# The up product's second pass on the two row halves of the TensorE array

## The chip, the cores and the metric

One core of a Trainium2 chip runs the kernel, in one launch. The metric is the device time of that launch in microseconds (us). The kernel before was run three times: 2138.86, 2139.70 and 2140.49 us, with a median of 2139.7 us.

## The reference

Four batches of 12480 queries, keys and values with 128 channels attend through 49 agents; the result, 49920 tokens of 128 channels, goes through a feed-forward layer with 2048 hidden values:

```
a2k = softmax(scale * agents @ k.T)        # 49 x 12480, per batch
agent_v = a2k @ v                          # 49 x 128
q2a = softmax(scale * q @ agents.T)        # 12480 x 49
x = q2a @ agent_v                          # 12480 x 128
h = x @ w_in                               # 128 -> 2048
out = (h * sigmoid(1.702 * h)) @ w_out     # 2048 -> 128
```

All of it is float32 (the feed-forward weights come as float64).

## The kernel before, in words

The kernel never forms `x`. Per batch it multiplies `agent_v` and `w_in` beforehand (`agent_weights`, L289 to L309): the product, 49 x 2048, is the weight matrix of the up product, and the queries' probabilities over the agents are its moving operand. The 49 agents are padded to 64 rows (`H`), and the weights stand twice on the 128 partitions, in rows 0 to 63 and again in rows 64 to 127.

To keep float32's accuracy with TensorE's `float32r` operands, values are split in an upper and a lower part. The weights become `wh` and `wl` (L307, L308). The probabilities of a group of 960 tokens, in two chunks of 480, become `sa` for the first chunk and `sb` for the second (`query_pairs`, L336 to L354). In `sa` the upper parts lie in rows 0 to 63 and the lower parts in rows 64 to 127; in `sb` it is the other way round. So one matmul over 128 rows sums upper and lower parts against the same weights.

The main loop (L540) has 4 batches x 13 groups x 16 blocks of 128 hidden values, 832 steps in all. A step is:

- `up`, four matmuls of 128 rows, 128 columns of weights and 480 columns of moving data: `wh` against `sa` and `sb` (L362), then `wl` against `sa` and `sb` (L364), summed in two PSUM tiles `ph`, one for each chunk. ScalarE applies the gate (L369) to give `g`; ScalarE or VectorE makes its upper part `gh` (L371, L373), VectorE the lower part `gl` (L374).
- `down`, for the block of four steps earlier (`LAG`), six matmuls of the same size (L385): `wo_h` against `gh`, `wo_h` against `gl`, `wo_l` against `gh`, for each chunk, summed in `po` over the 16 blocks.

So a step has ten matmuls of 128 x 128 x 480, each with its own load of 128 x 128 weights. Beside the steps, at fixed blocks of a group, come the next group's query scores (bfloat16 matmuls, L182 to L185), transposes of the probabilities (L345), and for the next batch key scores, key maxima (`key_max`, with the transposes L235 and L241) and key-value products (L272). L241 takes 49 rows and is one of only four matmuls of the kernel before with so few rows; the program gives it a tile of 64 x 128 of the array. The transpose L235 and the first batch's L489 have 49 columns of weights and a tile of 128 x 64; all others take 128 x 128.

The order on each engine is made by the tile scheduler from the order of the code and from the buffers. On TensorE the two matmuls of a line usually stand next to each other, but in some steps other work comes between. TensorE works through its instructions in the order of the program, and a weight load may run beside the matmul before it.

Of the kernel before, what the change touches and what calls it, by code (L numbers as in the profile page):

```python
# [20 lines left out]
CH = 480  # L21
# [21 lines left out]
def kernel(  # L43
# [10 lines left out]
    nc = tc.nc  # L54
# [6 lines left out]
    H = P // 2  # L61
# [9 lines left out]
    ps_o = ctx.enter_context(tc.tile_pool(name="ps_o", bufs=1, space=bass.MemoryType.PSUM))  # L71
    ps_m = ctx.enter_context(tc.tile_pool(name="ps_m", bufs=2, space=bass.MemoryType.PSUM))

# [1 line left out]
    ag_sb = const.tile([P, B, A], F32, name="ag_sb")  # L75
    nc.sync.dma_start(out=ag_sb, in_=agT)

    ident = const.tile([P, P], F32, name="ident")
    make_identity(nc, ident)
    # sel[k, m] = 1 where k and m name the same agent in either half  # L80
    sel = const.tile([P, P], F32, name="sel")
    nc.vector.memset(sel, 0.0)
    for c in range(2):
        nc.vector.tensor_add(
            out=sel[:, c * H : c * H + A], in0=ident[:, 0:A], in1=ident[:, H : H + A]
# [20 lines left out]
    part_max = const.tile([P, NKG, A], F32, name="part_max")  # L106
    max_b = const.tile([P, A], F32, name="max_b")

    # a float64's words, low then high, to the nearest float32; what is under
    # float32's range becomes zero and what is over it infinite  # L110
    def load_words(src, i):
        w = loads.tile([P, 512, 2], U32, name="words", tag="kv")
        nc.sync.dma_start(out=w.rearrange("p n w -> p (n w)"), in_=src[:, i * 1024 : (i + 1) * 1024])
        return w

    def to_float32(w, out=None):
        lo = w[:, :, 0]
        hi = w[:, :, 1]
        ts = nc.vector.tensor_scalar
        stt = nc.vector.scalar_tensor_tensor  # L120
        # 2 ** exponent, with the sign
        tmp = work.tile([P, 2, 512], U32, name="tmp", tag="rest")
        ex = tmp[:, 0].bitcast(I32)
        ts(out=ex.bitcast(U32), in0=hi, scalar1=20, scalar2=0x7FF, op0=ALU.logical_shift_right, op1=ALU.bitwise_and)
        ts(out=ex, in0=ex, scalar1=1023 - 127, scalar2=1023 + 128, op0=ALU.max, op1=ALU.min)
        ts(out=ex, in0=ex, scalar1=float(127 - 1023), scalar2=float(1 << 23), op0=ALU.add, op1=ALU.mult)
        stt(out=ex.bitcast(U32), in0=hi, scalar=0x80000000, in1=ex.bitcast(U32), op0=ALU.bitwise_and, op1=ALU.bitwise_or)
        # the mantissa's upper 45 bits as a whole number, rounded once
        m = work.tile([P, 512], U32, name="m21", tag="o")
        r = tmp[:, 1]  # L130
        ts(out=m, in0=hi, scalar1=0xFFFFF, scalar2=0x100000, op0=ALU.bitwise_and, op1=ALU.bitwise_or)
        ts(out=r, in0=lo, scalar1=8, scalar2=None, op0=ALU.logical_shift_right)
        stt(out=m.bitcast(F32), in0=m, scalar=float(1 << 24), in1=r, op0=ALU.mult, op1=ALU.add)
        if out is None:
            out = m.bitcast(F32)
        stt(out=out, in0=m.bitcast(F32), scalar=2.0**-44, in1=ex.bitcast(F32), op0=ALU.mult, op1=ALU.mult)
        return out

    def up_weights(i, w):
        to_float32(w, w_in_sb[:, i * 512 : (i + 1) * 512])  # L140

    def down_weights(i, w):
        s = slice(i * 4, (i + 1) * 4)
        wo = to_float32(w).rearrange("p (f c) -> p f c", c=C)
        nc.scalar.copy(out=wo_h[:, s, :], in_=wo)
        nc.vector.tensor_sub(out=wo_l[:, s, :], in0=wo, in1=wo_h[:, s, :].bitcast(F32))

    # ---- scores: a float32 is the sum of three bfloat16, and of the parts'
    # products all are summed but those under a float32 product's own rounding ----
    ag_part = const.tile([P, B, 3, A], BF16, name="ag_part")  # L150
    rest = ag_sb
    for i in range(3):
# [7 lines left out]
        w = t.bitcast(BF16).rearrange("p (n w) -> p n w", w=2)  # L160
        return w[:, :, 1], w[:, :, 0]

    # the upper half of a word is the first part; of what is left the upper
    # half is the second, and the third takes the place of the lower
    def split(t):
        r = work.tile([P, GT + PAD], F32, name="rest", tag="rest")
        nc.gpsimd.memset(t[:, GT:], 0.0)  # L167
        nc.gpsimd.tensor_sub(out=r, in0=t, in1=halves(t)[0])  # L168
        nc.gpsimd.tensor_sub(out=halves(r)[1], in0=r, in1=halves(r)[0])  # L169
        return halves(t)[0], halves(r)[0], halves(r)[1]  # L170
# [20 lines left out]
                nc.scalar.copy(out=o, in_=s[:, :, 0, :])  # L191
                nc.vector.tensor_add(out=o, in0=s[:, :, 1, :], in1=o)

# [1 line left out]
    def key_load(b, g):  # L195
        t = loads.tile([P, GT + PAD], F32, name="kt", tag="kv")
        nc.sync.dma_start(out=t[:, 0:GT], in_=kT[b, :, g * KB : (g + 1) * KB, :].rearrange("p j t -> p (j t)"))
        return t

    def first_key_scores(g, kt):  # L200
        # two batches' agents to a pass, as many columns as keep the clock up
        for c in range(2):
            ps = ps_m.tile([P, 512], F32, name="ps_m")
            for j in range(KB // 2):
                nc.tensor.matmul(  # L205
                    out=ps[:TB, j * 2 * A : (j + 1) * 2 * A],
                    lhsT=kt[:, c * KB // 2 + j, :],
                    rhs=ag_sb[:, 0:2, :].rearrange("p b a -> p (b a)"),
                    start=True,
                    stop=True,  # L210
                )
            s = ps[:TB, : KB * A].rearrange("p (j b a) -> p j b a", b=2, a=A)[:, :, 0, :]
            i = 2 * g + c
            nc.scalar.copy(out=score[:TB, i * KB // 2 : (i + 1) * KB // 2, :], in_=s)
        nc.vector.tensor_reduce(
            out=part_max[:TB, g, :],
            in_=score[:TB, g * KB : (g + 1) * KB, :].rearrange("p j a -> p a j"),
            axis=AX.X,
            op=ALU.max,
        )  # L220
# [87 lines left out]
            nc.vector.tensor_sub(out=wl[:, s], in0=pw, in1=wh[:, s].bitcast(F32))  # L308
        return wh, wl  # L309

# [1 line left out]
    def query_load(b, g):  # L312
        t = loads.tile([P, GT + PAD], F32, name="qt", tag="qt", bufs=2)
        nc.sync.dma_start(out=t[:, 0:GT], in_=qT[b, :, g * GT : (g + 1) * GT])
        return t
# [37 lines left out]
        nc.vector.tensor_sub(out=sb[0:H], in0=ps[H:P, :CH], in1=sb[H:P].bitcast(F32))  # L353
        return sa, sb  # L354

# [1 line left out]
    def up(f, wts, pairs):  # L357
        wh, wl = wts
        s = slice(f * P, (f + 1) * P)
        ph = [ps_h.tile([P, 512], F32, name="ph") for _ in range(2)]  # L360
        for c in range(2):
            nc.tensor.matmul(out=ph[c][:, :CH], lhsT=wh[:, s], rhs=pairs[c], start=True, stop=False)  # L362
        for c in range(2):
            nc.tensor.matmul(out=ph[c][:, :CH], lhsT=wl[:, s], rhs=pairs[c], start=False, stop=True)  # L364
        g = gpool.tile([P, 2, CH], F32, name="g")
        gh = gpool.tile([P, 2, CH], F32R, name="gh", bufs=LAG + 1)
        gl = gpool.tile([P, 2, CH], F32R, name="gl", bufs=LAG + 1)
        for c in range(2):
            nc.scalar.activation(out=g[:, c, :], in_=ph[c][:, :CH], func=AF.Gelu_apprx_sigmoid)  # L369
        if f in HI_ON_ACT:  # L370
            nc.scalar.copy(out=gh, in_=g)  # L371
        else:
            nc.vector.tensor_copy(out=gh, in_=g)  # L373
        nc.vector.tensor_sub(out=gl, in0=g, in1=gh.bitcast(F32))  # L374
        return gh, gl
# [21 lines left out]
            t0 = b * N + g * GT + c * CH  # L397
            nc.sync.dma_start(out=outT[:, t0 : t0 + CH], in_=o)

# [1 line left out]
    kts = {}  # L401
    vts = {}
    qts = {}
# [5 lines left out]
    pairs = {}  # L409
# [41 lines left out]
    def do_weights(b):  # L451
        wts[b] = agent_weights(accs.pop(b))

    # the first batch's keys and values have nothing to run beside, and lie
    # where the weights and the hidden values come to lie afterwards
    def first_keys():
        tags = [("g", 3), ("gh", LAG + 1), ("gl", LAG + 1)]
        tiles = []
        for tag, bufs in tags:
            tiles += [gpool.tile([P, KB, TB], F32, name="kt0", tag=tag, bufs=bufs) for _ in range(bufs)]  # L460
        return tiles[:NKG]
# [14 lines left out]
    words = [load_words(w_out, i) for i in range(NF // 4)]  # L476
    for g in range(NKG):
        first_key_scores(g, kts.pop((0, g)))
# [5 lines left out]
    for g in range(NKG):  # L484
# [3 lines left out]
        for j in range(KB):  # L488
            nc.tensor.matmul(  # L489
                out=acc_ps[:A, : C + 1],  # L490
                lhsT=score[:TB, g * KB + j, :],
                rhs=vt[:TB, j, :],
                start=(g == 0 and j == 0),
                stop=(g == NKG - 1 and j == KB - 1),
# [10 lines left out]
    do_weights(0)  # L505
    down_weights(0, words[0])

    # what is done for the next batch beside a group: in steps of the group's
    def beside(b, g):
        jobs = {}  # L510
        if b == 0 and g == 0:
# [25 lines left out]
    steps = B * NG * NF  # L537
# [70 lines left out]
```

## Time and profile before

| | us |
|---|---|
| median of three runs | 2139.7 |
| profiled execution, first to last instruction | 2139.6 |
| PE (TensorE matmul) busy | 2083.2 |
| PEld (TensorE weight load) busy | 1777.1 |
| DVE (VectorE) busy | 1865.0 |
| ACT (ScalarE) busy | 1611.9 |
| POOL (GpSimd) busy | 519.8 |

The profiled execution's own time is the span of 2139.6 us; the median of the runs is the same within 0.1 us. Busy time on PE is the time covered by matmul records. A record lasts from the issue to a modelled end, so records of matmuls that follow each other overlap: the time that a matmul takes from the stream is the distance between starts, not its record's length. L385 is line 385 of the kernel.

### The profile page before, as it was taken

To read this page: it belongs to the slowest core of one execution; us is meant where nothing else is said; L and a number is where in the kernel's file an instruction comes from. 1 tells how busy PE (TensorE), PEld (TensorE's weight loads), DVE (VectorE), ACT (ScalarE), POOL (GpSimd) and SP (SyncE) were. 2 spreads that over 40 slices of the span, in tenths; PEclk is the share of its full clock that TensorE was granted. 3 is DMA by queue.
4 is the path that set the end of the run, shared out by engine and by line. 5 is a ranking of instruction groups with operands and counts; after the bars stand their busy time and mean duration, and the time that the engine had idled before them with its cause. 6 is when DMAs were issued, how large, how long until landed. Compare 5 with 4: busy or idle time off the path is not lost.

```text
span 2139.6 us, 31613 instructions
## 1 busy us (share of the span) xinstructions
PE 2083.2 (97%) x12232; PEld 1777.1 (83%) x12232; DVE 1865.0 (87%) x2142; ACT 1611.9 (75%) x2590; POOL 519.8 (24%) x383
## 2 busy tenths in 40 slices
PE   8889989999999999999999999999999999999999
PEld 8678878888888887788888888778888888888887
DVE  6998998999889899899888899899898887888876
ACT  3567768977777776987777777798777877778786
POOL 4143445121123433421113342531110101001000
PEclk9999999999999999999999999999999999999999
DMA  9411221211111212112101212111100101010000
GB/s 265 119 48 49 65 73 38 61 48 50 38 38 47 66 47 56 47 56 56 56 20 47 63 49 56 55 51 53 47 19 19 38 19 38 19 38 20 25 14 19
DMA packets 49339, 108.57 MB, mean 51 GB/s; under 512 B 4252, under 2 KB 30172, under 8 KB 49188
## 3 DMA queue, kind: packets, MB, share of 16 engines
q1 hardware_dynamic: 49188, 106.55, 17.2%
q8 instruction: 96, 1.57, 0.3%
q14 instruction: 55, 0.45, 0.1%
HBM read 80.97 MB, written 25.56 MB: 50 GB/s over the span
## 4 chain that ended last, share of the span: by engine, by line
PE 81%; DVE 11%; issue 3%; ACT 3%; POOL 1%; DMA 1%; ACTq 0%; SPq 0%; DVEq 0%; POOLq 0%
PE po L385 43%; PE ph L362 15%; PE ph L364 14%; DVE gl L374 5%; DVE gh L373 2%; PE ps_m L272 1%; PE ps_m L182 1%; PE ps_m L184 1%; POOL score L251 1%; PE ps_m L205 1%; ACT g L369 1%; PE ps_m L345 1%; PE ps_m L306 1%; PE ps_m L183 1%; PE ps_m L185 1%
## 5 line engine op out<-in xcount | busy, mean ns | idle before, releaser
L374 DVE TENSOR_TENSOR gl<-g,gh 128x960 fp32r<-128x960 f32 x832 | 1034.4, 1258 | 189.4 <-ACT gh L371 174.3
L369 ACT ACTIVATE g<-ph 128x480 f32<-128x480 f32 x1664 | 855.2, 573 | 380.5 <-PE ph L364 265.7
L385 PE MATMUL po<-gl,wo_h 128*128 128x480 f32 x1664 | 501.9, 382 | 5.4 <-DVE gl L374 5.4
L385 PE MATMUL po<-gh,wo_h 128*128 128x480 f32 x1664 | 506.1, 383 | 0.7 <-ACT gh L371 0.7
L385 PE MATMUL po<-gh,wo_l 128*128 128x480 f32 x1664 | 501.6, 383 | 0.0
L371 ACT CAST gh<-g 128x960 fp32r<-128x960 f32 x416 | 416.0, 1000 | 10.9
L385 PEld LDWEIGHTS po<-gl,wo_h 128*128 128x128 f32 x1664 | 313.1, 189 | 60.0 <-DVE gl L374 9.2
L385 PEld LDWEIGHTS po<-gh,wo_h 128*128 128x128 f32 x1664 | 313.5, 189 | 53.2 <-ACT gh L371 1.1
L385 PEld LDWEIGHTS po<-gh,wo_l 128*128 128x128 f32 x1664 | 313.8, 189 | 49.9
L362 PE MATMUL ph<-sa,wh 128*128 128x480 f32 x832 | 332.5, 400 | 4.8 <-ACT g L369 4.8
L364 PE MATMUL ph<-sa,wl 128*128 128x480 f32 x832 | 319.3, 384 | 0.0
L362 PE MATMUL ph<-sb,wh 128*128 128x480 f32 x832 | 318.8, 383 | 0.0
L364 PE MATMUL ph<-sb,wl 128*128 128x480 f32 x832 | 316.6, 381 | 0.0
L373 DVE CAST gh<-g 128x960 fp32r<-128x960 f32 x416 | 298.6, 718 | 7.0 <-ACT g L369 6.6
L167 POOL MEMSET qt<- 128x8 f32 x52 | 5.7, 110 | 939.2 <-PE ps_m L185 472.0
L169 POOL TENSOR_TENSOR rest<-rest 128x968 bf16<-128x968 f32 x91 | 188.6, 2072 | 7.1
L362 PEld LDWEIGHTS ph<-sa,wh 128*128 128x128 f32 x832 | 157.7, 190 | 31.7 <-ACT g L369 10.8
L362 PEld LDWEIGHTS ph<-sb,wh 128*128 128x128 f32 x832 | 158.0, 190 | 26.6 <-ACT g L369 6.2
L364 PEld LDWEIGHTS ph<-sb,wl 128*128 128x128 f32 x832 | 156.9, 189 | 25.6 <-issue 1.0
L364 PEld LDWEIGHTS ph<-sa,wl 128*128 128x128 f32 x832 | 157.1, 189 | 24.7 <-issue 1.0
L168 POOL TENSOR_TENSOR rest<-qt 128x968 f32<-128x968 f32 x52 | 110.7, 2129 | 167.8 <-DMA qt<-qT 110.8
L184 PE MATMUL ps_m<-ag_part,rest 128*128 128x98 bf16 x728 | 110.2, 205 | 0.0
(103 smaller groups left out, 2077.8 us busy)
## 6 DMA issues: line engine op xcount, KB each, us to landing
kt<-kT SPq DMA_DIRECT2D x52, 480.0 KB, 3.6
qt<-qT SPq DMA_DIRECT2D x52, 480.0 KB, 3.8
vt<-v SPq DMA_DIRECT2D x52, 480.0 KB, 4.3
outT<-o SPq DMA_DIRECT2D x104, 240.0 KB, 2.2
words<-w_in SPq DMA_DIRECT2D x4, 512.0 KB, 10.9
words<-w_out SPq DMA_DIRECT2D x4, 512.0 KB, 8.2
ag_sb<-agT SPq DMA_DIRECT2D x1, 98.0 KB, 2.1
```

What stands on the lines that cost most here:

```text
L168: nc.gpsimd.tensor_sub(out=r, in0=t, in1=halves(t)[0])
L169: nc.gpsimd.tensor_sub(out=halves(r)[1], in0=r, in1=halves(r)[0])
L182: mm(out=o, lhsT=x0[:, t], rhs=a[:, 0 : 2 * A], start=True, stop=False)
L183: mm(out=o[:, A:], lhsT=x0[:, t], rhs=a[:, 2 * A :], start=False, stop=False)
L184: mm(out=o, lhsT=x1[:, t], rhs=a[:, 0 : 2 * A], start=False, stop=False)
L362: nc.tensor.matmul(out=ph[c][:, :CH], lhsT=wh[:, s], rhs=pairs[c], start=True, stop=False)
L364: nc.tensor.matmul(out=ph[c][:, :CH], lhsT=wl[:, s], rhs=pairs[c], start=False, stop=True)
L369: nc.scalar.activation(out=g[:, c, :], in_=ph[c][:, :CH], func=AF.Gelu_apprx_sigmoid)
L371: nc.scalar.copy(out=gh, in_=g)
L373: nc.vector.tensor_copy(out=gh, in_=g)
L374: nc.vector.tensor_sub(out=gl, in0=g, in1=gh.bitcast(F32))
L385: nc.tensor.matmul(out=po[c][:, :CH], lhsT=lhsT[:, f, :], rhs=rhs[:, c, :], start=(f == 0 and first), stop=(f == NF - 1 and last),)
```

## The change

In `up`, the matmuls with `wl` take 64 of the 128 rows. For the first chunk they are rows 0 to 63 of `wl` and of `sa`, for the second rows 64 to 127 of `wl` and of `sb`: the rows in which the upper parts of the probabilities lie. `tile_position` puts the first on the upper half of the array's rows and the second on the lower half, so that in the program each has a tile of 64 x 128, at rows 0 and 64. The product of the weights' lower parts and the probabilities' lower parts is no longer part of the sum. Each matmul still has 128 columns of weights, 480 columns of moving data and its own weight load.

```diff
         for c in range(2):
             nc.tensor.matmul(out=ph[c][:, :CH], lhsT=wh[:, s], rhs=pairs[c], start=True, stop=False)
         for c in range(2):
-            nc.tensor.matmul(out=ph[c][:, :CH], lhsT=wl[:, s], rhs=pairs[c], start=False, stop=True)
+            r = slice(c * H, (c + 1) * H)
+            nc.tensor.matmul(
+                out=ph[c][:, :CH], lhsT=wl[r, s], rhs=pairs[c][r], start=False, stop=True, tile_position=(c * H, 0)
+            )
```

The rest of the diff takes out comments. The matmul of L364 stands at L367 afterwards, that of L385 at L390. No instruction moves on any engine: the order of the kernel changed is that of the kernel before, with these line numbers. Two places of it matter below. On TensorE, early in the first group, a step in which the two matmuls of L367 stand next to each other (`ph` are the up product's sums, `po` those of the down product; a row names the output's size, not the rows that are taken):

```order
L390 MATMUL po_776<-gh,wo_l 128x480
L362 MATMUL ph<-sa,wh 128x480
L362 MATMUL ph<-sb,wh 128x480
L367 MATMUL ph<-sa,wl 128x480
L367 MATMUL ph<-sb,wl 128x480
L390 MATMUL po_775<-gh,wo_h 128x480
```

The two half-height matmuls follow each other here, with full-height ones on both sides. A little later, a step in which the scheduler has put the second chunk's first pass between them:

```order
L390 MATMUL po_775<-gh,wo_h 128x480
L362 MATMUL ph<-sa,wh 128x480
L367 MATMUL ph<-sa,wl 128x480
L362 MATMUL ph<-sb,wh 128x480
L367 MATMUL ph<-sb,wl 128x480
L390 MATMUL po_776<-gh,wo_h 128x480
```

Here each half-height matmul stands alone between full-height ones. Counted over the program, 789 runs hold at least one pair side by side (790 pairs, since one run holds two), and 84 matmuls, from 42 steps, stand alone.

## The prediction

> **What bounds the kernel now.** I read the page first, the shares of the engines, the chain that ended last and the costliest groups:
>
> ```profile
> span 2139.6 us, 31613 instructions
> PE 2083.2 (97%) x12232; PEld 1777.1 (83%) x12232; DVE 1865.0 (87%) x2142; ACT 1611.9 (75%) x2590; POOL 519.8 (24%) x383
> ...
> PE 81%; DVE 11%; issue 3%; ACT 3%; POOL 1%; DMA 1%; ACTq 0%; SPq 0%; DVEq 0%; POOLq 0%
> PE po L385 43%; PE ph L362 15%; PE ph L364 14%; DVE gl L374 5%; DVE gh L373 2%; PE ps_m L272 1%; PE ps_m L182 1%; PE ps_m L184 1%; POOL score L251 1%; PE ps_m L205 1%; ACT g L369 1%; PE ps_m L345 1%; PE ps_m L306 1%; PE ps_m L183 1%; PE ps_m L185 1%
> ...
> L364 PE MATMUL ph<-sa,wl 128*128 128x480 f32 x832 | 319.3, 384 | 0.0
> ...
> L364 PE MATMUL ph<-sb,wl 128*128 128x480 f32 x832 | 316.6, 381 | 0.0
> ```
>
> The reader is to see that TensorE makes up 81% of the chain, and that the 2 x 832 matmuls of L364, which the change touches, are 14% of it. VectorE, busy for 1865 us, is the next engine. Busy time is not the stream's time, though, since records overlap. So I then read the table by stretches, to see whether TensorE binds all along (columns: stretch, length, then the busy time of PE, PEld, DVE, ACT and POOL, granted clock, DMA share, GB/s):
>
> ```profile
> 300.00:1500.00 1200.00, 1179.66 (x7002) 1005.71 (x7002) 1083.52 (x1226) 935.78 (x1488) 350.28 (x243) 0.99 0.17 50
> 1500.00:2000.00 500.00, 500.00 (x2697) 426.67 (x2696) 416.66 (x476) 394.11 (x635) 54.10 (x44) 1.00 0.09 29
> ```
>
> It does, from 300 us to the end of these stretches, at a granted clock of 0.99 to 1.00. Last I read the timeline, in which the starts give what a matmul takes from the stream:
>
> ```profile
> 756.41 0.39 PE L362 MATMUL ph<-sa,wh 128*128 128x480 f32 x1
> 756.63 0.38 PE L362 MATMUL ph<-sb,wh 128*128 128x480 f32 x1
> 756.63 0.19 PEld L364 LDWEIGHTS ph<-sa,wl 128*128 128x128 f32 x1
> 756.85 0.38 PE L364 MATMUL ph<-sa,wl 128*128 128x480 f32 x1
> 756.86 0.19 PEld L364 LDWEIGHTS ph<-sb,wl 128*128 128x128 f32 x1
> ...
> 757.08 0.38 PE L364 MATMUL ph<-sb,wl 128*128 128x480 f32 x1
> 757.08 0.19 PEld L385 LDWEIGHTS po<-gh,wo_h 128*128 128x128 f32 x1
> ```
>
> Starts lie 0.22 us apart (756.63, 756.85, 757.08). Each load of weights begins when the matmul ahead of it starts, one ahead, and is covered by that matmul's streaming. A step of ten such matmuls takes 2.2 us of the 2139.6 / 832 = 2.57 us per step; most of the rest is scores, transposes and key work on TensorE. So what is added to or taken from TensorE's stream here shows in the time almost whole.
>
> **What the change removes.** Two matmuls of 0.22 us become two on different rows. If both stream at the same time, a pair takes one slot and 0.22 us goes; if the second can't begin before the first is done, nothing goes. Columns streamed and weight columns loaded stay the same, 480 and 128, so I leave the length of each at what it was. The pairs that stand side by side number 790, so at most 790 x 0.22 = 174 us go. The 84 matmuls that stand alone have no partner and save nothing.
>
> **What it adds.** Between full-height and half-height matmuls the array changes its tile. The kernel before does this mid-stream at one line, L241, a transpose of 49 rows with a 64 x 128 tile, between L364 and L385, both of the full 128 x 128:
>
> ```profile
> 328.78 0.21 DVE L239 COPY mrow<-mcol 49x120 f32<-49x120 f32 x1
> ...
> 328.94 0.37 PE L364 MATMUL ph<-sb,wl 128*128 128x480 f32 x1
> ...
> 329.24 0.13 PEld L241 LDWEIGHTS ps_m<-ident,mrow 49*120 49x120 f32 x1 [0.33 <-PE ph L364]
> 329.24 0.25 PE L241 MATMUL ps_m<-ident,mrow 49*120 49x49 f32 x1
> 329.43 0.30 PEld L385 LDWEIGHTS po<-gh,wo_h 128*128 128x128 f32 x2
> 329.43 0.70 PE L385 MATMUL po<-gh,wo_h 128*128 128x480 f32 x2
> 329.75 0.19 PEld L385 LDWEIGHTS po<-gl,wo_h 128*128 128x128 f32 x1
> ```
>
> Its operand was there at 328.78 + 0.21 = 328.99, yet its weights did not start to load under L364's matmul: they started at 329.24, 0.30 us after that matmul's start, which is 0.08 more than a slot. Behind it the same: L385's first load waits until L241 has run, 329.43, instead of starting with it. It then stands bare: the second matmul of L385 starts at 329.43 + 0.70 - 0.38 = 329.75, so the first took 0.32 instead of 0.22 us, 0.10 more. How long a bare load is without any change of tile is seen after the transposes of L345, whose streams are short:
>
> ```profile
> 406.24 0.24 PEld L345 LDWEIGHTS ps_m<-ident,p_pad 120*128 120x128 f32 x2
> 406.44 0.19 PEld L362 LDWEIGHTS ph<-sa,wh 128*128 128x128 f32 x1
> 406.47 0.46 PE L362 MATMUL ph<-sa,wh 128*128 128x480 f32 x1
> 406.55 0.19 PEld L362 LDWEIGHTS ph<-sb,wh 128*128 128x128 f32 x1
> ```
>
> The next load follows at 406.55, 0.11 us after 406.44. So I read a change of tile as two parts: about 0.08 us in which the array empties, and 0.11 us for the load that could not be drawn ahead; 0.19 us together. The emptying on the way back to full height can't be read apart from L241's own stream, and I take the same. The program has 789 + 84 = 873 runs of half-height matmuls, each with a change in and one out: 1746 changes x 0.19 = 332 us.
>
> The lower bound comes from the same rows. From L364's start to the second L385's is 329.75 - 328.94 = 0.81 us; less two slots of 0.22, the visit of L241 took 0.37 with its own work in it. That work is at most a slot of L345, about 0.10 (its two loads at 406.24 and the next at 406.44: two slots in 0.20). So two changes cost at least 0.27, and the 873 visits 236 us. The upper bound is what I took, since 2 x 0.19 is already 0.38.
>
> The Trainium skill speaks against this change: "TensorEngine Tiling (Array Packing)", Key Properties, says that changing the tiling mode, and not just the tile, drains TensorE. It gives no time for the drain; the late loads around L241 agree with it, and by it every one of these runs pays twice.
>
> **How much of the pair overlaps.** No row shows two half-height matmuls, so the saving lies between 0 and 0.22 us. Full-height loads go one ahead, since there the next load starts only with the matmul ahead of it (756.85 and 756.86). After L241 the bare load and its matmul are issued together, both at 329.43, and what holds the next load is that it wants the same rows. The second half's load wants other rows, so I take it to start right behind the first's, and the pair to take one slot: the whole 0.22, 174 us. That is the nearest row read one way; the other reading, one load after the other, is a rival below.
>
> The Trainium skill, "TensorE: Matmul & The Clock Gate", Part 3, gives about 4 ns from the start of one packed tile to the next. By that the 790 pairs would save 3 us less than I take; no row of the kernel before shows it.
>
> **What gives some back.** TensorE now waits at times for slower engines, and it would wait less if it were later itself:
>
> ```profile
> PEld ph L362 <- ACT g L369: 17.0, 58, 2.0
> PEld L182 <- DVE sb L353: 10.8, 5, 4.0
> PEld po L385 <- DVE gl L374: 9.2, 11, 2.6
> ```
>
> These are 37 us; I take half, 18 us, as swallowed. VectorE, ScalarE and the queues get the same instructions as before and more time for them.
>
> **The sum**, against the profiled execution's 2139.6 us (the median, 2139.7, is the same): +332 - 174 - 18 = +140, so 2280 us.
>
> **The rivals.**
>
> *The second half loads after the first.* If the array takes one load at a time whatever the rows, the second matmul starts 0.11 us late and a pair saves 0.11: 87 us instead of 174. For it: no two loads of the kernel before overlap in what they hold up. Time: 2139.6 + 332 - 87 - 18 = 2367 us.
>
> *The halves don't overlap at all.* Then the change only adds: 2139.6 + 332 - 18 = 2454 us. Nothing in the trace speaks for or against it, as no row has two tiles.
>
> *Faster: the array changes height without stopping.* L241 is a transpose, a rare one, and also carries a wait on VectorE, so its late loads may be its own. If ordinary matmuls change tile for nothing and pairs stream together, 174 us go: 2139.6 - 174 = 1966 us, with VectorE's 1865 us close behind. The point that decides is the price of a change: 174 / 1746 = 0.10 us. Below it the kernel gets faster. Against it stands that the bare load after L241, 0.10 us on an ordinary matmul, is alone as large.
>
> The Trainium skill's "TensorEngine Tiling (Array Packing)", Theoretical Speedup, gives up to 2x for a dimension of 64 or less. Applied to these pairs without any drain it is this rival.
>
> *Loads are drawn ahead after all, only the emptying stays.* 1746 x 0.08 = 140 us against 174: 2139.6 + 140 - 174 = 2106 us. Against it: none of the loads around L241 was drawn ahead.
>
> **How the numbers follow.** My forecast gets 0.44, the late second load 0.25, no overlap 0.15, the free change 0.10, the mere emptying 0.04; 0.02 is left for no change, where price and saving cancel. Faster is thus 0.10 + 0.04 = 0.14, the same 0.02, slower 0.44 + 0.25 + 0.15 = 0.84. About 0.2%, 4 us, is what a measurement of this kernel can tell from no change. The predicted time is the forecast's, 2280 us. With the lower price of the changes it would be 2139.6 + 236 - 174 - 18 = 2184; I go half way there, to 2230, and up past the rival without overlap, 2475, which leaves out the faster cases and part of the cheap end.
>
> **What would show it.** In the profile after, the first load of L367 should start some 0.3 us after the start of the last full-height matmul, and the first load of L390 should start only after the pair. The two matmuls of L367 should start within 0.02 us of each other; 0.11 apart is the first rival, 0.22 the second. Loads that start with the matmul ahead of them at the border would prove the forecast wrong, and the time would be below 2140. From the last full-height start to the first slot after the pair, I expect 0.22 + 0.08 + 0.11 + 0.22 + 0.08 + 0.11 = 0.82 us with the load, where 0.66 stood before. VectorE's busy time should stay near 1865 us, at a smaller share.

## The result and the profile after

The changed kernel took 2266.5 us (median of four runs, 2262.0 to 2269.0), the kernel before in the same comparison 2139.3 us: a ratio of 1.059, with a 95% interval of 1.0574 to 1.0606. It is slower by 127 us, as forecast, and 14 us faster than the 2280 us predicted. The profiled execution of the changed kernel spans 2260.2 us, 120.6 more than that of the kernel before.

The page after, its shares, its chain and the two groups of the second pass, now L367:

```profile
span 2260.2 us, 31613 instructions
PE 2233.8 (99%) x12232; PEld 1560.3 (69%) x12232; DVE 1855.1 (82%) x2142; ACT 1627.1 (72%) x2590; POOL 525.7 (23%) x383
...
PE 93%; DVE 4%; DMA 1%; ACT 1%; issue 1%; POOL 0%; ACTq 0%; SPq 0%; DVEq 0%; POOLq 0%
...
L367 PE MATMUL ph<-sa,wl 64*128 64x480 f32 x832 | 399.5, 480 | 0.0
L367 PE MATMUL ph<-sb,wl 64*128 64x480 f32 x832 | 399.5, 480 | 0.0
```

TensorE's share of the chain went from 81% to 93%, VectorE's from 11% to 4%, and VectorE's busy time hardly moved. Weight loads are busy for 217 us less although there are as many: busy time is time covered, and for the most part it is the two loads of a pair that now cover the same time. That is read from the timeline of one step of the changed kernel, a pair between full-height matmuls:

```profile
757.15 0.38 PE L362 MATMUL ph<-sb,wh 128*128 128x480 f32 x1
...
757.46 0.18 PEld L367 LDWEIGHTS ph<-sa,wl 64*128 64x128 f32 x1 [0.34 <-issue]
757.46 0.48 PE L367 MATMUL ph<-sa,wl 64*128 64x480 f32 x1
757.46 0.18 PEld L367 LDWEIGHTS ph<-sb,wl 64*128 64x128 f32 x1
757.46 0.48 PE L367 MATMUL ph<-sb,wl 64*128 64x480 f32 x1
757.87 0.30 PEld L390 LDWEIGHTS po<-gh,wo_h 128*128 128x128 f32 x2 [0.22 <-issue]
757.87 0.71 PE L390 MATMUL po<-gh,wo_h 128*128 128x480 f32 x2
```

The pair's first load starts 0.31 us after the last full-height matmul, where a slot is 0.22. Both loads and both matmuls start at 757.46. L390's load waits for the pair's end at 757.87, 0.41 later: 0.11 of load, 0.22 of streaming, 0.08 of emptying. Its second matmul starts at 757.87 + 0.71 - 0.38 = 758.20, 0.33 after the first. From 757.15 to 758.20 are 1.05 us; the same four intervals took 4 x 0.22 = 0.88 before. So a pair costs 0.17 us net, and with the slot it saves, its two changes of tile cost 0.17 + 0.22 = 0.39. Over all 779 pairs of the trace that have such full-height matmuls around them, the median way is 1.05 us too. And none of the 1746 loads at a change of height starts more than 0.03 us ahead of its own matmul, where a load between full-height matmuls starts about 0.22 ahead.

The Trainium skill, "TensorE: Matmul & The Clock Gate", Part 3, has packed tiles start about 4 ns apart; this trace agrees, within the 0.01 us that its rows show (757.46 for both).

TensorE's waits are shorter. These rows of the chart of waits are of the changed kernel (total, times, longest, in us):

```profile
PEld ph L362 <- ACT g L374: 7.4, 26, 0.6
PEld po L390 <- DVE gl L379: 3.7, 15, 0.3
...
PEld L182 <- DVE sb L353: 1.2, 1, 1.2
...
PEld ps_m L241 <- issue: 0.9, 1, 0.9
```

The first three stood at 17.0, 9.2 and 10.8 us before. The fourth, the wait ahead of the key maximum's transpose, before:

```profile
PEld ps_m L241 <- issue: 8.5, 3, 3.8
```

The mean granted clock, before and then after:

```profile
core 0: 2139.6 us, clock 0.992
```

```profile
core 0: 2260.2 us, clock 0.997
```

### The profile page after: what moved, and what is told of

Same layout as the page of the kernel before. It is cut to its first block, busy times and chain, and to the rows that moved or that the text cites. A ratio compares the mean times of both kernels' runs of the same rounds, so it can differ in the third digit from the quotient of the medians.

```text
span 2260.2 us, 31613 instructions
## 1 busy us (share of the span) xinstructions
PE 2233.8 (99%) x12232; PEld 1560.3 (69%) x12232; DVE 1855.1 (82%) x2142; ACT 1627.1 (72%) x2590; POOL 525.7 (23%) x383
## 4 chain that ended last, share of the span: by engine, by line
PE 93%; DVE 4%; DMA 1%; ACT 1%; issue 1%; POOL 0%; ACTq 0%; SPq 0%; DVEq 0%; POOLq 0%
PE po L390 53%; PE ph L362 16%; PE ph L367 15%; DVE gl L379 2%; PE ps_m L272 1%; PE ps_m L182 1%; PE ps_m L184 1%; PE ps_m L205 1%; PE ps_m L345 1%; PE ps_m L183 1%; PE ps_m L185 1%; PE ps_m L306 1%; DVE gh L378 0%; DMA words<-w_out 0%; POOL score L251 0%
## 5 line engine op out<-in xcount | busy, mean ns | idle before, releaser
L390 PE MATMUL po<-gh,wo_h 128*128 128x480 f32 x1664 | 589.2, 433 | 0.1
L390 PE MATMUL po<-gl,wo_h 128*128 128x480 f32 x1664 | 501.6, 381 | 0.0
L390 PE MATMUL po<-gh,wo_l 128*128 128x480 f32 x1664 | 499.9, 382 | 0.0
L376 ACT CAST gh<-g 128x960 fp32r<-128x960 f32 x416 | 414.0, 995 | 10.8
L367 PE MATMUL ph<-sa,wl 64*128 64x480 f32 x832 | 399.5, 480 | 0.0
L367 PE MATMUL ph<-sb,wl 64*128 64x480 f32 x832 | 399.5, 480 | 0.0
L390 PEld LDWEIGHTS po<-gh,wo_h 128*128 128x128 f32 x1664 | 250.6, 188 | 187.7 <-issue 178.5
L390 PEld LDWEIGHTS po<-gl,wo_h 128*128 128x128 f32 x1664 | 312.0, 188 | 53.9 <-issue 3.0
L390 PEld LDWEIGHTS po<-gh,wo_l 128*128 128x128 f32 x1664 | 312.6, 188 | 50.4 <-issue 0.5
L367 PEld LDWEIGHTS ph<-sa,wl 64*128 64x128 f32 x832 | 152.0, 183 | 278.5 <-issue 278.5
L378 DVE CAST gh<-g 128x960 fp32r<-128x960 f32 x416 | 291.1, 700 | 32.5 <-ACT g L374 32.3
L367 PEld LDWEIGHTS ph<-sb,wl 64*128 64x128 f32 x832 | 151.9, 183 | 9.9 <-issue 9.7
```

Of the source, the lines that this page charges most:

```text
L367: nc.tensor.matmul(out=ph[c][:, :CH], lhsT=wl[r, s], rhs=pairs[c][r], start=False, stop=True, tile_position=(c * H, 0))
L390: nc.tensor.matmul(out=po[c][:, :CH], lhsT=lhsT[:, f, :], rhs=rhs[:, c, :], start=(f == 0 and first), stop=(f == NF - 1 and last),)
```

## The experiments

My theory: each run of half-height matmuls pays twice for a change of tile, about 0.39 us together, and a pair saves one slot because its halves stream at the same time. Rivals: the overlap is only in the records, whose ends are modelled; fewer rows are slow by themselves; or each half-height pair is dear, whatever stands around it.

**Both on one half.** The pair keeps its height but shares its rows, so it can't overlap:

```diff
-            r = slice(c * H, (c + 1) * H)
+            r = slice(0, H)
             nc.tensor.matmul(
-                out=ph[c][:, :CH], lhsT=wl[r, s], rhs=pairs[c][r], start=False, stop=True, tile_position=(c * H, 0)
+                out=ph[c][:, :CH], lhsT=wl[r, s], rhs=pairs[c][r], start=False, stop=True, tile_position=(0, 0)
             )
```

> Both matmuls of the second pass take rows 0 to 63, so the second chunk's second pass multiplies the weights' lower parts with the probabilities' lower parts instead of the upper ones: that part of the sum is changed. Changes of tile stay as they are in the changed kernel (873 runs). My theory: the pair of the changed kernel streams at the same time, and on one half it can't, so 790 pairs lose 0.22 us each: 2266 + 172 = 2438 us. Rival (the overlap is only in the records, whose ends are modelled): no change, 2266 us.

Measured: 2419.9 us, 153 above the changed kernel, 19 short of the theory's 172. The timeline of a pair:

```profile
1003.54 0.37 PE L362 MATMUL ph<-sb,wh 128*128 128x480 f32 x1
1003.84 0.18 PEld L367 LDWEIGHTS ph<-sa,wl 64*128 64x128 f32 x1 [0.33 <-issue]
1003.84 0.48 PE L367 MATMUL ph<-sa,wl 64*128 64x480 f32 x1
1003.95 0.19 PEld L367 LDWEIGHTS ph<-sb,wl 64*128 64x128 f32 x1
1004.17 0.38 PE L367 MATMUL ph<-sb,wl 64*128 64x480 f32 x1
1004.48 0.30 PEld L390 LDWEIGHTS po<-gh,wo_h 128*128 128x128 f32 x2 [0.34 <-issue]
```

On the same rows the second load waits for the first, 0.11 us, and the second matmul for a slot; L390 comes 0.64 us after the pair's start instead of 0.41. The overlap on two halves is real: had it been in the records alone, the time would have stayed. Added up over the trace, the ways from a second-pass matmul's start to the next start, another of its pass or L390, are 514 us here and 342 in the changed kernel: the 172 us are there, and what came back came back elsewhere.

**A small matmul, full and half height.** The kernel before, with one more matmul ahead of each step's first pass. Here it is with half height; the full-height twin has `0:P` for `0:H`:

```diff
         ph = [ps_h.tile([P, 512], F32, name="ph") for _ in range(2)]
+        nc.tensor.matmul(
+            out=ph[0][:, CH:512], lhsT=wl[0:H, s], rhs=pairs[0][0:H, 0 : 512 - CH], start=True, stop=True
+        )
```

> The kernel before, with one more matmul in each of the 832 steps ahead of the first pass: 128 rows, 32 columns of moving data, into 32 columns of the PSUM bank that nothing reads. Full height, no change of tile. My theory: it streams 0.01 us and leaves the next load bare, 0.11 us: 832 x 0.11 = 92 us, less what TensorE's waits swallow (up to 46 us): 2185 to 2231 us.

> The same small matmul with 64 rows, so that each step has one run of half height with next to no streaming: 832 x 2 changes of tile. My theory: the visit costs 0.09 + 0.10 + 0.01 + 0.09 + 0.11 = 0.40 us, 333 us in all, less up to 46 us: 2427 to 2473 us, some 240 above the full-height twin. Rival (a matmul of 64 rows is dear by its length, not by the change of tile): within 20 us of the full-height twin.

Measured: 2214.8 us at full height and 2431.4 at half height, against 2139.5 of the kernel before. Both lie within the theory's ranges; half height costs 217 us more than its twin, where the theory had some 240. The timeline at half height:

```profile
1001.13 0.61 PE L388 MATMUL po<-gh,wo_l 128*128 128x480 f32 x2
1001.67 0.18 PEld L361 LDWEIGHTS ph<-sa,wl 64*128 64x128 f32 x1 [0.34 <-issue]
1001.67 0.28 PE L361 MATMUL ph<-sa,wl 64*128 64x32 f32 x1
1001.88 0.19 PEld L365 LDWEIGHTS ph<-sa,wh 128*128 128x128 f32 x1
1001.88 0.49 PE L365 MATMUL ph<-sa,wh 128*128 128x480 f32 x1
1001.98 0.19 PEld L365 LDWEIGHTS ph<-sb,wh 128*128 128x128 f32 x1
1002.21 0.38 PE L365 MATMUL ph<-sb,wh 128*128 128x480 f32 x1
```

The twin, at the same place:

```profile
1000.19 0.19 PEld L361 LDWEIGHTS ph<-sa,wl 128*128 128x128 f32 x1
1000.41 0.18 PE L361 MATMUL ph<-sa,wl 128*128 128x32 f32 x1
1000.41 0.19 PEld L365 LDWEIGHTS ph<-sa,wh 128*128 128x128 f32 x1
1000.44 0.46 PE L365 MATMUL ph<-sa,wh 128*128 128x480 f32 x1
1000.52 0.19 PEld L365 LDWEIGHTS ph<-sb,wh 128*128 128x128 f32 x1
```

At full height both loads run ahead, at 1000.19 and 1000.41, each with the start of the matmul before it; only the load of L365, which takes 0.11 us (to 1000.52), outlasts the small stream that runs above it. At half height neither does. The second L388 starts at 1001.13 + 0.61 - 0.38 = 1001.36, the small matmul's load 0.31 later. L365's load starts only at 1001.88, 0.21 after that: 0.11 of load, 0.01 of stream, and the rest emptying, about 0.09. That is the way back to full height, which the prediction could not read apart from L241's own stream. These are ordinary matmuls with no wait of their own, so it was not the transpose in L241 that held the loads back.

**96 rows in the full tile.** Fewer rows, no change of tile:

```diff
-            nc.tensor.matmul(out=ph[c][:, :CH], lhsT=wl[:, s], rhs=pairs[c], start=False, stop=True)
+            r = slice(0, 96)
+            nc.tensor.matmul(out=ph[c][:, :CH], lhsT=wl[r, s], rhs=pairs[c][r], start=False, stop=True)
```

> The kernel before with 96 instead of 128 rows in the second pass, rows 0 to 95 for both chunks, in the full 128 x 128 tile; the products of rows 96 to 127 are left out of the sum. My theory (what costs is the change of tile, not the fewer rows): as the kernel before, 2135 to 2145 us. Rival (fewer rows cost by themselves): towards the changed kernel, above 2200 us.

Measured: 2140.7 us against 2140.9, a ratio of 0.9996 (0.9985 to 1.0006). The groups' mean records are 386 and 380 ns, where they were 384 and 381:

```profile
L365 PE MATMUL ph<-sa,wl 96*128 96x480 f32 x832 | 321.3, 386 | 0.0
...
L365 PE MATMUL ph<-sb,wl 96*128 96x480 f32 x832 | 316.3, 380 | 0.0
```

So 96 rows instead of 128 cost and save nothing by themselves; the change of tile costs. The Trainium skill, "TensorEngine Tiling (Array Packing)", Key Properties, says that a change of the tiling mode drains TensorE. The trace agrees, with 0.08 to 0.09 us of emptying. The larger part of the cost is the load of 0.11 us that can't go ahead.

**The pairs kept together.** The changed kernel, with the scheduler held to the order of the code for the second pass:

```diff
-            nc.tensor.matmul(
+            mm = nc.tensor.matmul(
                 out=ph[c][:, :CH], lhsT=wl[r, s], rhs=pairs[c][r], start=False, stop=True, tile_position=(c * H, 0)
             )
+            tc.keep_in_program_order(mm)
```

> The changed kernel with the pair of the second pass kept side by side: about 832 runs instead of 873 and 42 more pairs. My theory: 41 runs x 0.39 = 16 us and 42 x 0.22 = 9 us less, 2267 - 25 = 2242 us, if no new waits come of it. Rival (the singles cost no more than pairs): 2267 us.

Measured: 2246.6 us, 20 below the changed kernel where the theory had 25. The ratio to the kernel before, 1.0489 (1.0474 to 1.0505), lies below the changed kernel's whole interval. The single half-height matmuls cost about what the theory gives them.

**Two blocks at a time.** Half the runs of half height, with two pairs in most:

```diff
-            live[t] = up(f, wts[b], pairs[n])
+            if f % 2 == 1:
+                ph = up(f - 1, wts[b], pairs[n])
...
+        for f in (f0, f0 + 1):
+            s = slice(f * P, (f + 1) * P)
+            for c in range(2):
+                r = slice(c * H, (c + 1) * H)
+                mm = nc.tensor.matmul(
+                    out=ph[f][c][:, :CH], lhsT=wl[r, s], rhs=pairs[c][r], start=False, stop=True, tile_position=(c * H, 0)
+                )
+                tc.keep_in_program_order(mm)
```

Both blocks' first passes stand ahead of this, then come two blocks' down products, and the gate of both. The control has the full-height matmul in this place.

> The control of the next run: the up product of two blocks at a time, eight matmuls of full height (four with the upper, then four with the lower parts of the weights), then the down product of two earlier blocks. Same matmuls as the kernel before, other order. Theory and rival alike: about the kernel before, 2110 to 2200 us, as the order may add or remove waits for ScalarE.

> The same order, with the four matmuls of the lower parts in half height, kept side by side: 433 runs (399 of two pairs, 34 of one) instead of 873. My theory: 433 x 0.39 = 169 us for the changes of tile, 832 x 0.22 = 183 us saved, so 14 us less than the control, if the second pair's loads go under the first pair's streams; 30 us more than the control if they stand bare (399 x 0.11). Rival (each half-height pair costs by itself, by 0.15 us as in the changed kernel): some 127 us more than the control.

Measured: 2202.0 us for the control and 2196.8 at half height; ratios to the kernel before 1.0296 (1.0270 to 1.0322) and 1.0279 (1.0261 to 1.0296). The two can't be told apart, but the rival's 127 us is out: with the same 832 half-height pairs and half the changes of tile, the loss is gone. Out too are the 30 us more of a second pair's loads that stand bare. Whether the theory's 14 us less are there can't be told from these times, as waits can hide a gain as well as a loss. The new order itself costs 64 us. I took that for waits on the gate, and let ScalarE make the upper parts of the other blocks:

```diff
-HI_ON_ACT = (0, 2, 4, 6, 8, 10, 12, 14)
+HI_ON_ACT = (1, 3, 5, 7, 9, 11, 13, 15)
```

> The two-block order with half height as before, but with ScalarE making the upper parts gh of the odd blocks instead of the even ones, so that VectorE can begin after the first block's gate. 417 runs. My theory: VectorE's waits for the gate get shorter, and 416 x 0.05 = 21 us lie below the full-height twin; if the twin comes down to the kernel before, 2139, this one comes to about 2120. Rival (a two-pair run saves nothing): same as the twin.

> The full-height twin of that run: same order and same odd blocks on ScalarE, no change of tile. Both: between the kernel before and the first control, 2139 to 2202 us, lower the less VectorE waits.

Measured: 2175.4 us at half height and 2171.1 for the twin, 1.0159 (1.0144 to 1.0174) and 1.0122 (1.0098 to 1.0145). Both came down, but the 21 us between them did not come. The chart of waits of the half-height kernel:

```profile
PEld ph L364 <- ACT g L381: 49.3, 178, 1.8
PEld po L401 <- DVE gl L389: 46.1, 132, 0.9
```

and of the twin:

```profile
PEld ph L364 <- ACT g L378: 25.7, 104, 1.7
...
PEld po L398 <- DVE gl L386: 3.9, 6, 0.9
```

At half height TensorE's loads wait longer on both. A load's wait can lie under a running matmul and cost nothing, so I set the pages beside it: span less PE's busy time is 82.0 us at half height and 70.0 in the twin, and the granted clocks, 0.983 and 0.987 over the span, withhold some 9 us more at half height. That is 21 of the 25 us between the 21 that were to be saved and the 4 that were lost. So the last pair leaves out half of the work on the gate's upper and lower parts:

```diff
-            gh = gpool.tile([P, 2, CH], F32R, name="gh", bufs=LAG + 1)
-            gl = gpool.tile([P, 2, CH], F32R, name="gl", bufs=LAG + 1)
+            gh = gpool.tile([P, 1, CH], F32R, name="gh", bufs=LAG + 1)
+            gl = gpool.tile([P, 1, CH], F32R, name="gl", bufs=LAG + 1)
...
-                    rhs=rhs[:, c, :],
+                    rhs=rhs[:, 0, :],
```

> The last pair again with ScalarE and VectorE made lighter, to see whether the 21 us that the two-block runs should save were swallowed by waits for these engines: the upper and lower parts gh and gl are made for the first chunk only, and the down product takes them for both chunks (so the second chunk's output is that of the first; half of that work is left out). All matmuls stay. My theory: TensorE binds now, and half height lies 832 x 0.22 - 417 x 0.39 = 20 us below its full-height twin. Rival (a run of two pairs saves nothing on TensorE): within 5 us of the twin.

> The full-height twin with the same work left out. Both: below the kernel before, since TensorE no longer waits for the gate: 2080 to 2130 us.

Measured: 2086.4 us at half height (0.9744 of the kernel before, 0.9731 to 0.9758) and 2092.6 for the twin (0.9772, 0.9758 to 0.9785). Half height is 6 us lower, no run of one inside the range of the other. That is neither the theory's 20 nor clearly the rival's nothing. A run of two pairs in the half-height kernel shows the saving on TensorE's stream:

```profile
1601.52 0.37 PE L364 MATMUL ph<-sb,wh 128*128 128x480 f32 x1
1601.82 0.18 PEld L369 LDWEIGHTS ph<-sa,wl 64*128 64x128 f32 x1 [0.33 <-issue]
...
1601.82 0.18 PEld L369 LDWEIGHTS ph<-sb,wl 64*128 64x128 f32 x1
...
1601.93 0.19 PEld L369 LDWEIGHTS ph<-sa,wl 64*128 64x128 f32 x1
1601.93 0.19 PEld L369 LDWEIGHTS ph<-sb,wl 64*128 64x128 f32 x1
1602.14 0.37 PE L369 MATMUL ph<-sa,wl 64*128 64x480 f32 x1
1602.15 0.37 PE L369 MATMUL ph<-sb,wl 64*128 64x480 f32 x1
1602.44 0.30 PEld L401 LDWEIGHTS po<-gh,wo_h 128*128 128x128 f32 x2 [0.33 <-issue]
1602.45 0.71 PE L401 MATMUL po<-gh,wo_h 128*128 128x480 f32 x2
```

The second pair's loads go under the first pair's streams, 0.11 us after them. From 1601.52 to the second L401 at 1602.45 + 0.71 - 0.38 = 1602.78 are 1.26 us, where six slots are 6 x 0.218 = 1.31 by the median between starts in the twin. Over all 407 runs of this kind in the trace the median is 1.27: 0.04 us saved by a run, 16 us over 417, of which 6 reached the end. The other 10 show ahead of the first pass: the ways from a start of L401 or L364 to the next start of L364 add up to 348 us in this trace, and to 338 in the twin's (there L398 and L364). The wait of L364's loads for the gate stands at 34.3 us in the chart, in the twin at 18.7. So a run of two pairs does save time on TensorE, and here waits ahead of the first pass take most of it. That waits and clock also took the saving in the pair with all its work fits the sums above, but no run tests it.

## Why the prediction was right, and where it was off

**What binds.** Right: TensorE bound the kernel, and most of what was added to its stream came through: 121 us of some 166.

**The price of a change of tile.** Right in mechanism and nearly in size, from one matmul of one odd line: 0.19 us predicted, 0.39 / 2 = 0.195 measured. The emptying on the way back, which the prediction assumed to be equal, is nearly that, 0.09 us by the small matmul. The way from the last full-height start to the first slot after the pair, forecast as 0.82 us, is 758.20 - 0.22 - 757.15 = 0.83. The rivals of the free change and of the mere emptying are out by the same run, whose loads come late in both directions.

**The pair.** Right: both start at 757.46, and the whole slot goes. The second load doesn't come right behind the first, as the prediction took it, but with it. The rival of the late second load is what rows in common do, not two halves; no overlap at all is out by the run on one half.

**The sum of both.** With the measured price, 873 x 0.39 = 340 us less 174 saved is 166, where the prediction had 158. An error of 0.01 us in that price would be 9 us in the sum.

**What is given back.** This term was mis-sized: 18 us predicted. The profiled executions lie 120.6 us apart, so 166 - 121 = 45 us came back. The four rows of waits fell from 17.0 + 9.2 + 10.8 + 8.5 = 45.5 to 7.4 + 3.7 + 1.2 + 0.9 = 13.2 us, so 32 came back there, not half of 37. TensorE's idle time by the two pages, span less PE's busy time, fell about as much, from 56.4 to 26.4 us.

The clock is another part that the prediction left out: 0.8% of 2139.6 us were withheld before, 17 us, and 0.3% of 2260.2 after, 7 us. That makes 42 of 45, and the rest lies within the rounding of the price.

That the clock moves the time is seen in the four runs of the changed kernel: those at 0.997 took 2262.0 and 2264.1 us, those at 0.994 took 2268.9 and 2269.0. That the higher clock follows from the shorter waits was not tested. For it speaks where the clock was low: from 849 to 856 us of the kernel before it was 0.51, around and behind L241's wait of 3.8 us, which ended at 850.5. The longest waits of the four rows were 4.0 and 3.8 us before and are 1.2 and 0.9 now, and from 100 to 2000 us the changed kernel was granted 1.00.

**No version was faster.** With all the gate's work in place, the best of the half-height kernels, two blocks at a time, is 1.6% slower than the kernel before. Runs longer than two pairs were not tried: four PSUM tiles hold two blocks.

## What to carry to other kernels

Two matmuls on the two row halves of the array do run at the same time, but a run of them between full-height matmuls pays for two changes of tile: here 0.39 us against the 0.22 that a pair saves, so a run must hold two pairs to break even, and what is then left is small. A rare line of the old trace, here a transpose of 49 rows, can price an operation that the new kernel issues 1746 times: look for it before you sum. And when the binding engine gets slower, its waits for the others can shrink by more than half: here the four rows lost 32 of 45.5 us.

## What the runs showed of the hardware that was not expected

Loads for the two row halves run at the same time, in full: both start at 757.46, and with two pairs both second loads start together at 1601.93, while the first streams. On common rows the second load came 0.11 us later. A matmul of 96 rows takes as long as one of 128, within the 0.2% that the runs can tell, and makes no change of tile: 386 and 380 ns beside 384 and 381 in the mean records.
